# Entering the last feed-forward layer: item 0's activation ahead of a branch, and two items instead of three between the up and the down projection

## The chip, the core and the metric
The kernel runs on one core of a Trainium2 chip. The metric is the device time of one execution in microseconds (us), here the median of several runs. The engines are called as the profile calls them: PE (matrix multiply, with PEld for its weight loads), DVE (vector), ACT (scalar), POOL (GpSimd) and SP, which here only issues transfers. Each engine works through its own list of instructions in order, and waits for others by semaphores.

## What is computed
A cluster-masked attention (4 batches, 8 heads, 768 positions, 64 wide) is followed by a soft mixture of experts and by a feed-forward layer (FFN) with an odd activation:

```python
d = softmax over tokens of x @ phi;  slot_out = experts(d.T @ x)   # 32 slots of 512
x2 = softmax over slots(x @ phi) @ slot_out                         # 3072 x 512
h = x2 @ w_in                                                       # 512 -> 2048
g = h - tanh(h)
out = g @ w_out                                                     # 2048 -> 512
```

The change is at the entry of the last three lines and in their loop. The kernel never forms x2: it multiplies the 32 rows of slot_out with w_in first (`gp`, 32 x 2048), and then the softmax weights with that.

## The kernel before
The attention and the experts run to about 560 us; nothing in them is touched but the last copy of the expert outputs (`o_t`). Then the FFN works on 128 **items**: 8 groups of 384 tokens, and in each group 16 blocks `f` of 128 hidden units. For item n the work is, engine by engine:

- **up(n)**, PE, L1184: one matmul gives `u`, the 128 x 384 block of h. Its weights `gs` hold the 128 columns of block f as a high part twice and a low part (96 rows).
- **small(n)**, L1212 to L1223: ACT squares u to `y` and y to `z` (a shifted square, for a polynomial in h squared); DVE makes `gt` = u*y (L1216) and then gt = (z + c)*gt, a SCALAR_TENSOR_TENSOR that is called **STT** here (L1223). With large h another arm of the program also takes tanh itself; a flag that is computed on the chip chooses the arm (`big_h`), and in this run the arm without tanh works.
- **split(n)**, L1231 and L1233: ACT casts gt to a high part `ghi`, DVE subtracts to get the low part `glo`.
- **down(n)**, PE, L1243 to L1245: nine matmuls of 512 columns, for each of three token tiles ghi x whi, ghi x wlo and glo x whi, into the tile's accumulator `acc`. After 16 items ACT copies tiles 0 and 2 out and DVE tile 1 (`store`, L1252).

`up` and `down` of an item lie three rounds of the loop apart. In one round the order of the code is up(n), down(n-3), small(n-1), split(n-2), store(n-3).

During the first 16 items the weights are prepared too. `mix_g(q)` (PE, L1166) makes gp for four blocks; `gcopy(f)` copies it into gs (ACT L1172, then DVE L1177, and for the high part's second copy DVE L1176 in the first four blocks and POOL L1174 later); `wsplit(f)` makes `whi` on ACT (L1155) and `wlo` on POOL (L1156) from w_out. gp has one buffer, so mix_g(1) waits for the last copy of quarter 0. `u` has two PSUM buffers, ghi and glo three each.

Ahead of the branch stand mix_g(0), the flag (L1191 to L1199), gcopy(0) to (3) and wsplit(0) and (1); the arm begins with up(0).

Of the kernel before, what the change touches and what calls it, by code (L numbers as in the profile page):

```python
# [8 lines left out]
F32 = mybir.dt.float32  # L9
# [4 lines left out]
ACTF = mybir.ActivationFunctionType  # L14
ALU = mybir.AluOpType
# [313 lines left out]
def _poly():  # L329
    y = np.linspace(1e-6, H_CUT * H_CUT, 4001)  # L330
    h = np.sqrt(y)
    q = np.zeros_like(y)
    c = [1 / 3, -2 / 15, 17 / 315, -62 / 2835, 1382 / 155925, -21844 / 6081075, 929569 / 638512875]
    for k, a in enumerate(c):
        q += a * y ** k
    x = 2 * y / y[-1] - 1
    p = np.polynomial.chebyshev.cheb2poly(np.polynomial.chebyshev.chebfit(x, q, 2))
    s = 2 / y[-1]
    c2 = p[2] * s * s
    c1 = p[1] * s - 2 * p[2] * s  # L340
    c0 = p[0] - p[1] + p[2]
    r = np.sqrt(c2)
    t = c1 / (2 * r)
    return float(r), float(t), float(c0 - t * t)
# [3 lines left out]
def tile_cluster_attention_softmoe_ffn(  # L348
# [15 lines left out]
    PE, DVE, ACT, POOL, SP = nc.tensor, nc.vector, nc.scalar, nc.gpsimd, nc.sync  # L364
# [3 lines left out]
    DM = H * D  # L368
# [7 lines left out]
    HS = S // 2  # L376
    NT = S // 128
    NTOK = B * S
    KD = DM // 128
    KF = DFF // 128  # L380
    scale = 1.0 / float(D) ** 0.5
# [4 lines left out]
    keep = ctx.enter_context(tc.tile_pool(name="keep", bufs=1))  # L386
# [16 lines left out]
    ident, tri, istack, ones, afs, afb, eps, sq_b, lo_b = kviews  # L403
# [63 lines left out]
    POLY = _poly()  # L467
# [586 lines left out]
    ps_q = ctx.enter_context(tc.tile_pool(name="ps_q", bufs=1, space=PSUM, reuse_waits="tile"))  # L1054
# [26 lines left out]
    sot = keep.tile([128, KD, NS], F32, name="sot")  # L1081
# [28 lines left out]

    def o_t(gi, op):
        so = m1.tile([128, DM], F32, tag="hs", name="so")
        ACT.copy(out=so, in_=op)
        g = ps_m.tile([128, KD, 128], F32, tag="m", name="m")
        for d in range(KD):
            PE.transpose(g[:, d, :], so[:, d * 128:(d + 1) * 128], ident)
        for j in range(4):
            e = 4 * gi + j
            DVE.tensor_copy(sot[:, :, 4 * e:4 * e + 4], g[:, :, 32 * j + 4 * e:32 * j + 4 * e + 4])
# [15 lines left out]
    for f in range(F1 // 128):  # L1135
        o_mm(1, ops_[1], f)
        if f == 1:
            o_t(0, ops_[0])
        if f == 4:
            mix(3)  # L1140
    o_t(1, ops_[1])

    mctx.close()
# [4 lines left out]
    whi = ff.tile([128, KF, DM], F32R, name="whi")  # L1148
    wlo = ff.tile([128, KF, DM], F32R, name="wlo")
# [3 lines left out]
    def wsplit(f):  # L1153
        w = wu[NW + f // 4 * 4 + 2 + f // 2 % 2][:, (f % 2) * DM:(f % 2 + 1) * DM]
        ACT.copy(out=whi[:, f, :], in_=w)  # L1155
        POOL.tensor_tensor(out=wlo[:, f, :], in0=w, in1=whi.bitcast(F32)[:, f, :], op=ALU.subtract)  # L1156

    gq = {}

    def mix_g(q):  # L1160
        gq[q] = gp = ps_q.tile([128, 512], F32, tag="q", name="gp")
        for d in range(KD):
            for j in range(4):
                t = wu[NW + 4 * q + d // 2]
                c = (d % 2) * 512 + j * 128
                PE.matmul(gp[32 * j:32 * j + 32, 0:128], lhsT=sot[:, d, :], rhs=t[:, c:c + 128], start=(d == 0), stop=(d == KD - 1))  # L1166

    def gcopy(f):
        q, j = divmod(f, 4)
        fs = slice(f * 128, f * 128 + 128)  # L1170
        gpj = gq[q][32 * j:32 * j + 32, 0:128]
        ACT.copy(out=gs[0:32, fs], in_=gpj)  # L1172
        if q:
            POOL.tensor_copy(gs[32:64, fs], gf[0:32, fs])  # L1174
        else:
            DVE.tensor_copy(gs[32:64, fs], gpj)  # L1176
        DVE.tensor_tensor(out=gs[64:96, fs], in0=gpj, in1=gf[0:32, fs], op=ALU.subtract)  # L1177

    hps0 = {}

    def up(n, hps):
        g, f = items[n]
        hps[n] = ps_u.tile([128, HS], F32, tag="u", name="u")
        PE.matmul(hps[n], lhsT=gs[:, f * 128:(f + 1) * 128], rhs=cs[g // 2][0:96, g % 2 * HS:(g % 2 + 1) * HS], start=True, stop=True)  # L1184

    pctx.close()
    f3 = ctx.enter_context(tc.tile_pool(name="f3", bufs=3))
    ps_u = ctx.enter_context(tc.tile_pool(name="ps_u", bufs=2, space=PSUM, reuse_waits="tile"))
    ps_a = ctx.enter_context(tc.tile_pool(name="ps_a", bufs=5, space=PSUM, reuse_waits="tile"))
    ab = keep.tile([128, KD, NS], F32, name="ab")  # L1190
    ACT.activation(out=ab, in_=sot, func=ACTF.Abs)  # L1191
    bp = ps_a.tile([128, DM], F32, tag="acc", name="bp")
    mix_g(0)
    for d in range(KD):
        PE.matmul(bp[0:1, 0:NS], lhsT=md[:, d:d + 1], rhs=ab[:, d, :], start=(d == 0), stop=(d == KD - 1))
    bm = keep.tile([1, 1], F32, name="bm")
    DVE.tensor_reduce(out=bm, in_=bp[0:1, 0:NS], axis=AX.X, op=ALU.max)
    flag = keep.tile([1, 1], mybir.dt.int32, name="flag")
    DVE.tensor_scalar(out=flag, in0=bm, scalar1=H_CUT * (1.0 - 2.0 ** -12), scalar2=None, op0=ALU.is_gt)  # L1199
    for f in range(4):  # L1200
        gcopy(f)
        if f < 2:
            wsplit(f)
    big_h = nc.values_load(flag[0:1, 0:1], min_val=0, max_val=1)

    def ffn(any_h):
        hps, gts, gh, acc = dict(hps0), {}, {}, {}

        def small(n):
            hp = hps.pop(n)  # L1210
            y = f3.tile([128, HS], F32, tag="y", name="y", bufs=2)
            ACT.activation(out=y, in_=hp, func=ACTF.Square)  # L1212
            z = f3.tile([128, HS], F32, tag="z", name="z", bufs=2)
            ACT.activation(out=z, in_=y, func=ACTF.Square, scale=POLY[0], bias=sq_b)  # L1214
            gt = f3.tile([128, HS], F32, tag="gt", name="gt")
            DVE.tensor_tensor(out=gt, in0=hp, in1=y, op=ALU.mult)  # L1216
            if any_h:
                th = f3.tile([128, HS], F32, tag="th", name="th", bufs=1)
                ACT.activation(out=th, in_=hp, func=ACTF.Tanh)
                mk = f3.tile([128, HS], F32, tag="mk", name="mk", bufs=1)  # L1220
                POOL.tensor_scalar(out=mk, in0=y, scalar1=H_CUT * H_CUT, scalar2=None, op0=ALU.is_gt)
                DVE.tensor_tensor(out=th, in0=hp, in1=th, op=ALU.subtract)
            DVE.scalar_tensor_tensor(out=gt, in0=z, scalar=POLY[2], in1=gt, op0=ALU.add, op1=ALU.mult)  # L1223
            if any_h:
                DVE.copy_predicated(out=gt, mask=mk.bitcast(U32), data=th)
            gts[n] = gt

        def split(n):
            gt = gts.pop(n)
            a = f3.tile([128, HS], F32R, tag="ghi", name="ghi")  # L1230
            ACT.copy(out=a, in_=gt)  # L1231
            l = f3.tile([128, HS], F32R, tag="glo", name="glo")
            DVE.tensor_tensor(out=l, in0=gt, in1=a.bitcast(F32), op=ALU.subtract)  # L1233
            gh[n] = (a, l)

        def down(n):
            g, f = items[n]
            a, l = gh.pop(n)
            for t in range(3):
                if f == 0:  # L1240
                    acc[t] = ps_a.tile([128, DM], F32, tag="acc", name="acc")
                ts = slice(t * 128, (t + 1) * 128)
                PE.matmul(acc[t], lhsT=a[:, ts], rhs=whi[:, f, :], start=(f == 0), stop=False)  # L1243
                PE.matmul(acc[t], lhsT=a[:, ts], rhs=wlo[:, f, :], start=False, stop=False)  # L1244
                PE.matmul(acc[t], lhsT=l[:, ts], rhs=whi[:, f, :], start=False, stop=(f == KF - 1))  # L1245

        def store(n):
            g, f = items[n]
            if f == KF - 1:
                for t in range(3):  # L1250
                    ob = f3.tile([128, DM], F32, tag="ob", name="ob", bufs=3)
                    (DVE.tensor_copy if t == 1 else ACT.copy)(out=ob, in_=acc[t])  # L1252
                    r0 = g * HS + t * 128
                    SP.dma_start(out=out[r0:r0 + 128, :], in_=ob)

        N = len(items)
        for n in range(N + 4):
            if n < N:
                up(n, hps)
            if 4 <= n + 1 < KF:  # L1260
                gcopy(n + 1)
            if n >= 3 and n - 3 < N:
                down(n - 3)
            if 0 <= n - 1 < N:
                small(n - 1)
            if 0 <= n - 2 < N:
                split(n - 2)
            if n >= 3 and n - 3 < N:
                store(n - 3)
            if 2 <= n < KF:  # L1270
                wsplit(n)
            if n % 4 == 1 and n + 3 < KF:
                mix_g(n // 4 + 1)
# [65 lines left out]
```

## Time and profile before

| | |
|---|---|
| median of 3 runs | 861.09 us (860.93 to 864.15) |
| the profiled execution's own time | 866.37 us |
| its span, first to last instruction | 864.5 us |
| PE busy | 796.1 us (92%) |
| DVE, ACT, POOL busy | 600.5, 524.7, 396.8 us |
| mean granted clock of PE | 0.967 |

The profile is one execution, 5.3 us longer than the median; its times are measured from the first instruction. A row of the timeline gives start, duration, engine, line, operation, output <- inputs, shapes, and in brackets how long the engine had been idle and what ended that. A record can overlap the next one of its engine: the next starts while the last results are still being written.

### The profile page before, as it was taken

How to read it: one execution, taken by the hardware profiler on the slowest of the kernel's cores; microseconds unless marked ns; L12 is line 12 of the kernel's file. 1: busy time of each engine (PE TensorE's matmuls, PEld its weight loads, DVE VectorE, ACT ScalarE, POOL GpSimd, SP SyncE). 2: the span in 40 equal slices, each digit the busy share in tenths (PEclk: the TensorE clock that was granted, in tenths of full speed). 3: DMA queues.
4: the chain of work that ended last, by engine and by line, in shares of the span. 5: the costliest groups of instructions: out<-in, count | busy, mean ns of one | idle time of the engine just before them, and what ended most of it. 6: DMA issues, size and time to landing. Idle time of an engine off the chain costs nothing.

```text
span 864.5 us, 12652 instructions
## 1 busy us (share of the span) xinstructions
PE 796.1 (92%) x4327; PEld 543.5 (63%) x4327; DVE 600.5 (69%) x1017; ACT 524.7 (61%) x1085; POOL 396.8 (46%) x235
## 2 busy tenths in 40 slices
PE   1677899999999999999989979989999999999997
PEld 0343565666566656656666533368888888888885
DVE  2474676889778998789877551177767777677773
ACT  3253666658666576665656540288767767677673
POOL 1246668887887879887867721166000000000000
PEclk9798999999999999999989987989999999999999
DMA  8876788677767977678657689960000100000001
GB/s 219 187 189 174 175 230 242 170 185 186 219 174 177 220 174 205 194 201 208 181 179 275 243 341 388 382 228 2 37 37 1 38 0 38 37 1 37 1 37 40
DMA packets 49532, 135.13 MB, mean 156 GB/s; under 512 B 6866, under 2 KB 9350, under 8 KB 49460
## 3 DMA queue, kind: packets, MB, share of 16 engines
q1 hardware_dynamic: 42700, 116.29, 46.7%
q10 hardware_dynamic: 6760, 17.96, 6.9%
q8 instruction: 36, 0.59, 0.3%
q14 instruction: 36, 0.29, 0.1%
HBM read 78.55 MB, written 14.78 MB: 108 GB/s over the span
## 4 chain that ended last, share of the span: by engine, by line
PE 76%; DMA 9%; DVE 6%; SPq 3%; ACT 2%; issue 1%; POOL 1%; ACTq 0%; DVEq 0%; POOLq 0%
PE pv L671 12%; PE acc L1245 10%; PE acc L1243 10%; PE acc L1244 10%; PE st L658 7%; PE st L659 6%; PE g L605 6%; DMA pga<-in_qk_dram 4%; PE u L1184 3%; PE g L725 2%; PE h L1090 2%; DVE mx L613 2%; PE o L1109 2%; DMA xy<-pga 1%; DMA v<-in_vv_dram 1%
## 5 line engine op out<-in xcount | busy, mean ns | idle before, releaser
L676 POOL TENSOR_TENSOR es<-es,E 128x768 f32<-128x768 f32 x126 | 246.0, 1970 | 43.7 <-ACT E L663 35.8
L663 ACT ACTIVATE E<-st 128x384 f32<-128x384 f32 x384 | 174.9, 490 | 109.6 <-PE st L659 101.6
L613 DVE TENSOR_REDUCE mx<-g 128x1 f32<-128x512 f32 (+1 forms) x288 | 185.0, 682 | 69.4 <-PE g L605 68.4
L658 PE MATMUL st<-xy 112*128 112x384 f32 x384 | 146.9, 383 | 4.3 <-ACT E L663 4.3
L1245 PE MATMUL acc<-whi,glo 128*128 128x512 f32 x384 | 150.5, 392 | 0.0
L1243 PE MATMUL acc<-whi,ghi 128*128 128x512 f32 x384 | 150.2, 391 | 0.0
L1244 PE MATMUL acc<-wlo,ghi 128*128 128x512 f32 x384 | 150.0, 391 | 0.0
L671 PE MATMUL pv<-E,v 128*64 128x384 f32 x768 | 146.3, 505 | 0.0
L659 PE MATMUL st<-xy 97*128 97x384 f32 x384 | 132.0, 344 | 0.8 <-ACT xy L635 0.8
L605 PE MATMUL g<-xy 112*128 112x256 f32 (+1 forms) x384 | 104.6, 359 | 12.1 <-DMA xy<-pgb 8.5
L1216 DVE TENSOR_TENSOR gt<-u,y 128x384 f32<-128x384 f32 x128 | 71.2, 556 | 51.5 <-ACT y L1212 49.8
L658 PEld LDWEIGHTS st<-xy 112*128 112x128 f32 x384 | 73.7, 192 | 49.6 <-issue 20.5
L1212 ACT ACTIVATE y<-u 128x384 f32<-128x384 f32 x128 | 62.9, 492 | 57.5 <-PE u L1184 56.6
L671 PEld LDWEIGHTS pv<-E,v 128*64 128x64 f32 x768 | 47.7, 138 | 65.5 <-issue 62.3
L605 PEld LDWEIGHTS g<-xy 112*128 112x128 f32 x384 | 69.8, 198 | 23.3 <-issue 11.5
L1245 PEld LDWEIGHTS acc<-whi,glo 128*128 128x128 f32 x384 | 72.3, 188 | 17.8 <-DVE glo L1233 2.9
L1243 PEld LDWEIGHTS acc<-whi,ghi 128*128 128x128 f32 x384 | 72.7, 189 | 15.1
L495 POOL TENSOR_TENSOR pgb<-pga 128x768 fp32r<-128x768 f32 x31 | 58.4, 1889 | 51.6 <-DVE mx L613 24.1
L1214 ACT ACTIVATE z<-y,kt 128x384 f32<-128x384 f32 x128 | 79.2, 619 | 4.2
L1223 DVE SCALAR_TENSOR_TENSOR gt<-z,gt 128x384 f32<-128x384 f32 x128 | 71.9, 562 | 13.7 <-ACT ghi L1231 0.5
L676 POOL TENSOR_TENSOR es<-E 128x768 f32<-128x768 f32 x32 | 59.2, 1869 | 43.8 <-PE g L698 29.8
L1244 PEld LDWEIGHTS acc<-wlo,ghi 128*128 128x128 f32 x384 | 72.6, 189 | 10.2
(149 smaller groups left out, 948.8 us busy)
## 6 DMA issues: line engine op xcount, KB each, us to landing
pgw<-in_w_dram SPq DMA_DIRECT2D x64, 512.0 KB
xy<-pga SPq DMA_DIRECT2D x15, 768.0 KB
pga<-in_qk_dram ACTq DMA_DIRECT2D x14, 768.0 KB
pgc<-in_w_in_dram SPq DMA_DIRECT2D x8, 1024.0 KB
pgc<-in_w_out_dram SPq DMA_DIRECT2D x8, 1024.0 KB
xy<-pga SPq DMA_DIRECT2D x18, 384.0 KB
v<-in_vv_dram ACTq DMA_DIRECT2D x16, 384.0 KB
xy<-pga SPq DMA_DIRECT2D x32, 192.0 KB
```

What stands on the lines that cost most here:

```text
L605: PE.matmul(g[:, o:o + kn], lhsT=x[0:112, QX, qt * 128:(qt + 1) * 128], rhs=x[0:112, KX, k0:k0 + kn], start=True, stop=True)
L613: DVE.tensor_reduce(out=m[:, m0:m0 + w], in_=g.rearrange("p (a b) -> p a b", a=w), axis=AX.X, op=ALU.max)
L658: PE.matmul(s, lhsT=x[0:112, KX, ks], rhs=x[0:112, QX, qs], start=True, stop=False)
L659: PE.matmul(s, lhsT=x[0:97, KY, ks], rhs=x[0:97, QY, qs], start=False, stop=True)
L663: ACT.activation(out=et[p, kb, c][:, h, :], in_=s, func=ACTF.Exp, scale=scale)
L671: PE.matmul(pv[p, c][64 * h:64 * h + 64, :], lhsT=vt[p][:, kb, h, :], rhs=et[p, kb, c][:, h, :], start=(kb == 0), stop=(kb == NKB - 1))
L676: add_engine(p, kb, c).tensor_tensor(out=es[p][:, c], in0=et[p, 0, c] if kb == 1 else es[p][:, c], in1=et[p, kb, c], op=ALU.add)
L1214: ACT.activation(out=z, in_=y, func=ACTF.Square, scale=POLY[0], bias=sq_b)
L1223: DVE.scalar_tensor_tensor(out=gt, in0=z, scalar=POLY[2], in1=gt, op0=ALU.add, op1=ALU.mult)
L1243: PE.matmul(acc[t], lhsT=a[:, ts], rhs=whi[:, f, :], start=(f == 0), stop=False)
L1244: PE.matmul(acc[t], lhsT=a[:, ts], rhs=wlo[:, f, :], start=False, stop=False)
L1245: PE.matmul(acc[t], lhsT=l[:, ts], rhs=whi[:, f, :], start=False, stop=(f == KF - 1))
```

## The change
It has four parts, and the parts of the FFN's entry belong together.

1. wsplit(0) is issued before the flag's first step. The flag's last two steps come behind gcopy(0) on DVE, and up(0) and small(0) stand ahead of the branch, outside both arms. gcopy(2), gcopy(3) and wsplit(1) go into the arms.
2. gp is one tile, with 128 columns of its own for each quarter, so that mix_g(q) no longer waits for the copies of the quarter before it. In the built program ACT's copy gs(2) waits for the last matmul of mix_g(1).
3. A round of the loop is up(n), gcopy(n+1), down(n-2), split(n-1), small(n), store(n-2), wsplit(n). The nine matmuls of down(0) alone are sorted by kind: first the three ghi x whi.
4. In the second o_t, ACT copies the first half of the columns and DVE the second. In the built program DVE's half waits for ACT's.

```diff
     def o_t(gi, op):
         so = m1.tile([128, DM], F32, tag="hs", name="so")
-        ACT.copy(out=so, in_=op)
+        if gi:
+            ACT.copy(out=so[:, 0:DM // 2], in_=op[:, 0:DM // 2])
+            DVE.tensor_copy(so[:, DM // 2:DM], op[:, DM // 2:DM])
+        else:
+            ACT.copy(out=so, in_=op)
...
-    gq = {}
+    gq = ps_q.tile([128, 512], F32, tag="q", name="gp")
     def mix_g(q):
-        gq[q] = gp = ps_q.tile([128, 512], F32, tag="q", name="gp")
...
-                PE.matmul(gp[32 * j:32 * j + 32, 0:128], lhsT=sot[:, d, :], rhs=t[:, c:c + 128], start=(d == 0), stop=(d == KD - 1))
+                PE.matmul(gq[32 * j:32 * j + 32, q * 128:q * 128 + 128], lhsT=sot[:, d, :], rhs=t[:, c:c + 128], start=(d == 0), stop=(d == KD - 1))
...
+    wsplit(0)
     ACT.activation(out=ab, in_=sot, func=ACTF.Abs)
...
+    gcopy(0)
+    up(0, hps0)
     DVE.tensor_reduce(out=bm, in_=bp[0:1, 0:NS], axis=AX.X, op=ALU.max)
-    flag = keep.tile([1, 1], mybir.dt.int32, name="flag")
     DVE.tensor_scalar(out=flag, in0=bm, scalar1=H_CUT * (1.0 - 2.0 ** -12), scalar2=None, op0=ALU.is_gt)
-    for f in range(4):
-        gcopy(f)
-        if f < 2:
-            wsplit(f)
+    gcopy(1)
+    y0, z0, gt0 = y_z(0, hps0.pop(0), "gt0")
+    DVE.scalar_tensor_tensor(out=gt0, in0=z0, scalar=POLY[2], in1=gt0, op0=ALU.add, op1=ALU.mult)
     big_h = nc.values_load(flag[0:1, 0:1], min_val=0, max_val=1)
...
-        for n in range(N + 4):
+        if any_h:
+            up(0, hps)
+            small(0)
+        else:
+            gts[0] = gt0
+        up(1, hps)
+        mix_g(1)
+        split(0)
+        wsplit(1)
+        gcopy(2)
+        small(1)
+        for n in range(2, N + 2):
             if n < N:
                 up(n, hps)
-            if 4 <= n + 1 < KF:
+            if n + 1 < KF:
                 gcopy(n + 1)
-            if n >= 3 and n - 3 < N:
-                down(n - 3)
-            if 0 <= n - 1 < N:
-                small(n - 1)
-            if 0 <= n - 2 < N:
-                split(n - 2)
-            if n >= 3 and n - 3 < N:
-                store(n - 3)
-            if 2 <= n < KF:
+            down(n - 2)
+            if n <= N:
+                split(n - 1)
+            if n < N:
+                small(n)
+            store(n - 2)
+            if n < KF:
                 wsplit(n)
```

How the instructions stand is shown at three places. First PE at the branch (TENSOR_LOAD reads the flag), before:

```order
L1166 MATMUL gp<-pgw,sot 32x128 x16
L1195 MATMUL bp<-ab,md 1x32 x4
L1204 TENSOR_LOAD flag
L1275 COMPARE_AND_BRANCH
L1184 MATMUL u<-csm,gs 128x384 x2
L1166 MATMUL gp<-pgw,sot 32x128 x16
L1184 MATMUL u<-csm,gs 128x384 x2
L1243 MATMUL acc<-whi,ghi 128x512
```

And of the change:

```order
L1169 MATMUL gp<-pgw,sot 32x128 x16
L1199 MATMUL bp<-ab,md 1x32 x4
L1187 MATMUL u<-csm,gs 128x384
L1219 TENSOR_LOAD flag
L1295 COMPARE_AND_BRANCH
L1187 MATMUL u<-csm,gs 128x384
L1169 MATMUL gp<-pgw,sot 32x128 x16
L1187 MATMUL u<-csm,gs 128x384
L1256 MATMUL acc<-whi,ghi 128x512 x3
```

One up is now ahead of the branch, and three instead of four ups are ahead of the first down. The second place is DVE during the first 16 items; the numbers tell the buffers of one item from those of the next. Before:

```order
L1216 TENSOR_TENSOR gt_9959<-u_9914,y_9955 128x384
L1223 SCALAR_TENSOR_TENSOR gt_9959<-z_9957,gt_9959 128x384
L1233 TENSOR_TENSOR glo_9964<-gt_9932,ghi_9962 128x384
L1177 TENSOR_TENSOR gs_5750<-gp_9870,gs_5750 32x128
L1216 TENSOR_TENSOR gt_9986<-u_9941,y_9982 128x384
L1223 SCALAR_TENSOR_TENSOR gt_9986<-z_9984,gt_9986 128x384
L1233 TENSOR_TENSOR glo_9991<-gt_9959,ghi_9989 128x384
```

And of the change:

```order
L1209 TENSOR_TENSOR gt_9959<-u_9937,y_9955 128x384
L1233 SCALAR_TENSOR_TENSOR gt_9959<-z_9957,gt_9959 128x384
L1180 TENSOR_TENSOR gs_5751<-gp_5754,gs_5751 32x128
L1243 TENSOR_TENSOR glo_9980<-gt_9959,ghi_9978 128x384
L1209 TENSOR_TENSOR gt_9986<-u_9964,y_9982 128x384
L1233 SCALAR_TENSOR_TENSOR gt_9986<-z_9984,gt_9986 128x384
```

Before, the subtraction that reads gt_9959 (glo_9991) stands behind the whole next item's gt and STT; now it (glo_9980) stands ahead of them. The third place is ACT in the same items, before:

```order
L1231 CAST ghi_9962<-gt_9932 128x384
L1155 CAST whi_5751<-pgw_5492 128x512
L1172 CAST gs_5750<-gp_9870 32x128
L1212 ACTIVATE y_9982<-u_9941 128x384
L1214 ACTIVATE z_9984<-y_9982,kt_77 128x384
L1231 CAST ghi_9989<-gt_9959 128x384
```

And of the change:

```order
L1241 CAST ghi_9951<-gt_9932 128x384
L1205 ACTIVATE y_9955<-u_9937 128x384
L1207 ACTIVATE z_9957<-y_9955,kt_77 128x384
L1159 CAST whi_5752<-pgw_5485 128x512
L1175 CAST gs_5751<-gp_5754 32x128
L1241 CAST ghi_9978<-gt_9959 128x384
```

The cast of an item (ghi_9989 before, ghi_9978 now, both from gt_9959) used to follow y and z of the next item, and now stands ahead of them. The first 16 items are used for the place because whi and gs stand between there; behind them the order of ghi, y, z and of glo, gt, STT is the same without those.

## Rows read from the trace of the kernel before

**Rows 1.** The page's head.

```profile
span 864.5 us, 12652 instructions
```

**Rows 2.** Windows: start:end, length, busy (x instructions) of PE, PEld, DVE, ACT, POOL; clock; DMA.

```profile
567.00:573.00 6.00, 5.98 (x44) 4.35 (x37) 5.06 (x11) 5.80 (x14) 2.94 (x3) 0.58 1.05 383
650.00:700.00 50.00, 50.00 (x226) 41.73 (x225) 36.50 (x71) 35.02 (x70) 0.00 (x0) 1.00 0.04 17
```

**Rows 3.** Timeline of all engines, from the branch to the end of down(0).

```profile
564.14 0.41 PE L1184 MATMUL u<-csm,gs 96*128 96x384 f32 x1 [1.28 <-ACT gs L1172]
...
566.31 0.30 DVE L1177 TENSOR_TENSOR gs<-gp,gs 32x128 fp32r<-32x128 f32 x1
...
566.66 1.94 PE L1166 MATMUL gp<-pgw,sot 128*32 128x128 f32 x32 [1.33 <-DVE gs L1177]
...
568.16 0.56 DVE L1223 SCALAR_TENSOR_TENSOR gt<-z,gt 128x384 f32<-128x384 f32 x1
...
568.75 0.51 ACT L1231 CAST ghi<-gt 128x384 fp32r<-128x384 f32 x1
...
569.72 0.63 PE L1243 MATMUL acc<-whi,ghi 128*128 128x512 f32 x1
...
572.84 0.34 PE L1184 MATMUL u<-csm,gs 96*128 96x384 f32 x1
```

**Rows 4.** Timeline of ACT and DVE behind the first group's store.

```profile
608.85 0.59 ACT L1252 COPY ob<-acc 128x512 f32<-128x512 f32 x1 [0.77 <-PE acc L1245]
...
609.33 0.50 ACT L1212 ACTIVATE y<-u 128x384 f32<-128x384 f32 x1
609.86 0.56 DVE L1216 TENSOR_TENSOR gt<-u,y 128x384 f32<-128x384 f32 x1 [1.00 <-ACT y L1212]
...
610.39 0.50 ACT L1231 CAST ghi<-gt 128x384 fp32r<-128x384 f32 x1
...
610.53 0.56 DVE L1223 SCALAR_TENSOR_TENSOR gt<-z,gt 128x384 f32<-128x384 f32 x1
...
610.79 0.48 ACT L1212 ACTIVATE y<-u 128x384 f32<-128x384 f32 x1
...
611.00 0.55 DVE L1233 TENSOR_TENSOR glo<-gt,ghi 128x384 fp32r<-128x384 f32 x1
...
611.47 0.55 DVE L1216 TENSOR_TENSOR gt<-u,y 128x384 f32<-128x384 f32 x1
```

**Rows 5.** Timeline of one item in the middle of the FFN.

```profile
700.40 0.34 PE L1184 MATMUL u<-csm,gs 96*128 96x384 f32 x1
...
700.77 0.49 ACT L1212 ACTIVATE y<-u 128x384 f32<-128x384 f32 x1 [0.67 <-PE u L1184]
...
702.62 0.34 PE L1184 MATMUL u<-csm,gs 96*128 96x384 f32 x1
```

**Rows 6.** Timeline of one engine each: POOL and what DVE and ACT do beside it.

```profile
576.02 0.62 ACT L1155 CAST whi<-pgw 128x512 fp32r<-128x512 f32 x1
...
576.78 1.30 POOL L1156 TENSOR_TENSOR wlo<-pgw,whi 128x512 fp32r<-128x512 f32 x1 [0.32 <-ACT whi L1155]
...
599.96 0.55 DVE L1233 TENSOR_TENSOR glo<-gt,ghi 128x384 fp32r<-128x384 f32 x1
...
600.23 1.44 POOL L1156 TENSOR_TENSOR wlo<-pgw,whi 128x512 fp32r<-128x512 f32 x1 [0.60 <-ACT whi L1155]
...
601.34 0.75 DVE L1223 SCALAR_TENSOR_TENSOR gt<-z,gt 128x384 f32<-128x384 f32 x1
...
433.81 1.92 POOL L676 TENSOR_TENSOR es<-E 128x768 f32<-128x768 f32 x1
...
433.99 2.15 DVE L536 TENSOR_TENSOR eq<-pgb,am 128x384 bf16<-128x384 f32 x1
...
L536 DVE TENSOR_TENSOR eq<-pgb,am x16: 518/560/2152, 9.7 to 434.0; 128x384 bf16<-128x384 f32 x16
```

**Rows 7.** Timeline of PE, its last matmul.

```profile
858.21 0.39 PE L1245 MATMUL acc<-whi,glo 128*128 128x512 f32 x1
```

More of the change, by code (lines that the diff above doesn't have):

```diff
@@ L1170, in gcopy @@
         fs = slice(f * 128, f * 128 + 128)
-        gpj = gq[q][32 * j:32 * j + 32, 0:128]
+        gpj = gq[32 * j:32 * j + 32, q * 128:q * 128 + 128]
         ACT.copy(out=gs[0:32, fs], in_=gpj)
@@ L1196, in tile_cluster_attention_softmoe_ffn, with y_z @@
     bm = keep.tile([1, 1], F32, name="bm")
+    flag = keep.tile([1, 1], mybir.dt.int32, name="flag")
+    def y_z(n, hp, tag="gt"):
+        y = f3.tile([128, HS], F32, tag="y", name="y", bufs=2)
+        ACT.activation(out=y, in_=hp, func=ACTF.Square)
+        z = f3.tile([128, HS], F32, tag="z", name="z", bufs=2)
+        ACT.activation(out=z, in_=y, func=ACTF.Square, scale=POLY[0], bias=sq_b)
+        gt = f3.tile([128, HS], F32, tag=tag, name="gt", bufs=3 if tag == "gt" else 1)
+        DVE.tensor_tensor(out=gt, in0=hp, in1=y, op=ALU.mult)
+        return y, z, gt
+    gcopy(0)
+    up(0, hps0)
     DVE.tensor_reduce(out=bm, in_=bp[0:1, 0:NS], axis=AX.X, op=ALU.max)
-    flag = keep.tile([1, 1], mybir.dt.int32, name="flag")
     DVE.tensor_scalar(out=flag, in0=bm, scalar1=H_CUT * (1.0 - 2.0 ** -12), scalar2=None, op0=ALU.is_gt)
-    for f in range(4):
-        gcopy(f)
-        if f < 2:
-            wsplit(f)
+    gcopy(1)
+    y0, z0, gt0 = y_z(0, hps0.pop(0), "gt0")
+    DVE.scalar_tensor_tensor(out=gt0, in0=z0, scalar=POLY[2], in1=gt0, op0=ALU.add, op1=ALU.mult)
     big_h = nc.values_load(flag[0:1, 0:1], min_val=0, max_val=1)
@@ L1210, in small @@
             hp = hps.pop(n)
[L1211 to L1216, printed above, removed]
+            y, z, gt = y_z(n, hp)
             if any_h:
@@ L1238, in down @@
             a, l = gh.pop(n)
-            for t in range(3):
-                if f == 0:
+            if f == 0:
+                for t in range(3):
                     acc[t] = ps_a.tile([128, DM], F32, tag="acc", name="acc")
[L1242 to L1245, printed above, removed]
+            mms = [(t, k) for t in range(3) for k in range(3)]
+            if n == 0:
+                mms.sort(key=lambda m: m[1])
+            for t, k in mms:
+                PE.matmul(acc[t], lhsT=(l if k == 2 else a)[:, t * 128:(t + 1) * 128], rhs=(wlo if k == 1 else whi)[:, f, :], start=(f == 0 and k == 0), stop=(f == KF - 1 and k == 2))
         def store(n):
```

## The prediction, made before the change was run
> **What bounds the kernel now.** I read the page's head first: the span of the profiled execution is 864.5 us [rows 1], 1.87 short of its own 866.37, and that time is 5.3 above the median of 861.09. All sums below are made inside this execution, as a shift of its last matmul, and the shift is then added to the median. Next the windows: in the middle of the FFN PE is busy 50.00 of 50 us at a granted clock of 1.00, DVE 36.5 and ACT 35.0 [rows 2]. So PE is the bound there, and the item in the timeline takes 702.62 - 700.40 = 2.22 us [rows 5]. DVE and ACT have a quarter of the time free, but a busy share says nothing on how long they need one after the other. That is what the change touches, so the rest is read from timelines: the entry [rows 3], the hops between ACT and DVE [rows 4], POOL beside DVE [rows 6] and the end [rows 7].
>
> **The loop after the change.** Before, STT(n-1) stands ahead of glo(n-2) on DVE, and ghi(n-2) behind y and z of n-1 on ACT. An item crosses between the engines, but its split doesn't hold up the next item's STT. After it, ACT does ghi(n-1), y(n), z(n) and DVE glo(n-1), gt(n), STT(n). STT(n) therefore stands behind glo(n-1), which needs ghi(n-1), which needs STT(n-1): a closed loop, once around for each item. Its legs:
> - STT to ghi: 568.75 - 568.16 = 0.59 [rows 3].
> - ghi to glo: an ACT operation of 0.50 and the hop to DVE, as y at 609.33 to gt at 609.86, 0.53 [rows 4].
> - glo to gt on DVE: 611.47 - 611.00 = 0.47 [rows 4].
> - gt to STT, which reads it: 610.53 - 609.86 = 0.67 [rows 4].
>
> They sum to 2.26 (each is rounded to 0.01; I take 2.255), against PE's 2.22. y and z of n lie inside (y at 0.40 after ghi, 610.39 to 610.79, and 1.06 for y and z together, 609.33 to 610.39 [rows 4]), so ACT is ready when STT wants z. The loop becomes the bound by some 0.035 an item. From item 16 to 127 that is 111 turns, 250.3 us.
>
> **Group edges.** store's two ACT copies, 0.48 each (608.85 to 609.33 [rows 4]), now stand between z(n) and ghi(n). From ghi to ghi ACT then needs 0.40 + 1.06 + 0.96 = 2.42, 0.17 over 2.255. Seven edges make 1.2 us. Nothing hides it, since the loop has no slack.
>
> **The first 16 items.** There POOL works beside DVE, and two operations that read only SBUF hold each other up. The eq of L536 takes 0.56 in the median and 2.15 when it starts at 433.99 beside POOL's es (433.81 to 435.73); STT at 601.34 takes 0.75 in place of 0.56 beside wlo (600.23 to 601.67) [rows 6]. Both end about 0.41 after a point 0.15 ahead of POOL's end, as though they began there. The other way round, that wlo took 1.44 and not 1.30, with glo at 599.96 ahead of it. So a wlo holds a later STT or glo for about 1.15 after its start, and waits itself for about 0.41 after the start of an earlier one. gt and the copies into gs read PSUM and are not held in these rows. In before such a hold falls on an operation that isn't in a loop; now it lengthens the loop.
>
> wlo's place: y 0.40 after ghi, whi 1.06 behind, wlo 0.76 after whi (576.02 to 576.78 [rows 6]), so 2.22 after ghi or 2.81 after STT. Two patterns are possible.
> - **A**: STT is first, wlo gets in at STT + 0.41 and holds until + 1.56. glo, which is due at 0.59 + 0.53 = 1.12, starts at 1.56, gt at 2.03, STT at 2.69. The next wlo is due at 2.81, behind that STT again: this repeats, by a margin of 0.12, with a turn of 2.69.
> - **B**: wlo starts when STT has just ended (+ 0.56) and holds until 1.71; glo 1.71, gt 2.18, the next STT due at 2.84. The next wlo, due at 2.81, is 0.03 ahead and holds this STT to 3.96. The turn behind that is free again, 2.25. The mean is 3.1.
>
> Which runs hangs on 0.03 to 0.12 us, less than I can add up. I take the middle, 2.9, and keep 2.69 and 3.1 as bounds. Thirteen turns (items 3 to 16) make 37.7.
>
> The Trainium skill, in "SBUF — State Buffer", section "Who interferes with whom", says that a DVE instruction with two SBUF inputs and a GpSimd instruction that reads SBUF exclude each other for a whole instruction. The rows agree in kind and differ by 0.15 at the end; by the page a hold would last all of 1.30, pattern A would turn in 2.84, and the sum would be 13 x 0.15 = 2.0 us higher.
>
> **The entry.** u(0), y, z, gt and STT of item 0 now run while the flag is made and read. The flag comes behind two DVE copies of 0.30 each (566.31 [rows 3]), so the branch is about 0.6 late, and u(1) behind it starts at 564.14 + 0.6, about 564.8. mix_g(1) no longer waits for the last copy at 566.31 + 0.30; before it began at 566.66 and took 1.94 [rows 3]. Now it follows u(1) and ends at about 566.9. gs(2) waits for that: an ACT copy and two DVE copies, about 0.9, then hops; u(2) at about 567.9 and down(0) at 568.3, against 569.72 [rows 3]. PE is at the lower level there (granted clock 0.58 in 567 to 573 [rows 2]; 0.5 is 1.2 GHz): nine matmuls of 512 columns take 9 x 0.43 = 3.9, and u(3) starts at 572.2; with the 3.12 of before (569.72 to 572.84 [rows 3]) at 571.4. Before, the u that follows down(0) starts at 572.84, and PE has one u less left: u is 384 of an item's 4992 columns, 0.17. So the gain for PE is 0.5, and 1.3 at the other bound. This is all that the part can bring, however early item 0's activation is, since from there PE has a full list.
>
> Costed at nothing: wsplit(0) ahead of the absolute values (they are wanted only behind mix_g(0), 16 matmuls pairs on PE; uncovered it would be one ACT and one POOL operation, 0.76 and 1.30); the branch on ACT and DVE, beside PE's u(1) and mix_g(1); the order inside down(0), which lets PE start with ghi alone and whose nine matmuls are the same. The second o_t's halves are chained in the built program, ACT's and then DVE's, so its transposes start about when they did: 0, at most 0.1 either way. No transfer moves against another on SP.
>
> **The sum.** STT(3) is y + gt + STT behind u(3): 572.2 + 0.37 (700.40 to 700.77 [rows 5]) + 0.53 + 0.67 = 573.8. Then 37.7, 250.3 and 1.2 give STT(127) at 863.0. The end: ghi 0.59, glo 0.53, 0.55 for it [rows 4] and a hop of 0.05 (566.31 + 0.30 to 566.66 [rows 3]) to the third matmul, and six more of 2.22 x 512/4992 = 0.23: 3.1. The last matmul starts at 866.1, against 858.21 [rows 7]: + 7.9. On the median, 861.1 + 7.9 = **868.9 us** (874.2 for a profiled execution like this one). With A alone it is 866.2, with B alone 871.5.
>
> **Rivals.**
> - **No hold in the loop**: STT and glo slip in between wlo's, because wlo comes later than 2.81, behind the gs copies on ACT and POOL. Then the weight stage goes at PE's pace, 2.22 and two mix_g of some 0.97 (half of 1.94 at the full clock) over 13 items, 2.37. 13 turns are 30.8, the last matmul 859.2, + 1.0: 862.1. For it: STT at 601.34 lost only 0.19. Against: wlo needs 1.3 of every turn, and glo and STT are 1.13 to 1.7 apart, so there is hardly a gap that it fits.
> - **PE stays the bound** (the other side): the loop turns in 2.22 or less, because a leg is 0.04 shorter when nothing else is in flight, and holds eat only the slack. Then the entry's 0.5 to 1.3 is all that is left: 859.8 to 860.6, not slower. It is decided at a turn of 2.22. Against: four rows would have to be wrong in the same direction, and the holds fall in the first 16 items even so; for: PE can trail, as ghi and glo are ready some 1.7 us ahead of their down.
> - **The clock comes back sooner**: with down(0) 1.4 us earlier and fewer gaps ahead of it, nine matmuls at the full clock would take 2.05 and not 3.9, 1.8 less: 867.1 by my sum, 858.4 if PE is the bound too.
>
> **How the numbers follow.** The loop with holds, A, B or a mixture: 0.63, 865 to 872. No hold in the loop: 0.20, near 862. PE the bound: 0.12, 858.4 to 860.6. Something longer than B: 0.05. The early clock (0.25, in any of them) shifts each by less than 2. The range of 861 to 872 leaves out about 0.15. A measurement of this kernel tells some 0.5%, 4.3 us, from no change: faster is under 856.8, which only PE as the bound, an early clock and edges that get cheaper together would reach, 0.04; slower is above 865.4, most of the first case and the last, 0.63; the rest 0.33.
>
> **What would show it.** Between 650 and 700 us u's start 2.25 to 2.26 apart, PE has gaps that glo or ghi end, and its busy time falls under 50; if they are 2.22 apart, the loop isn't the bound. Between 572 and 610 STT or glo rows of 0.9 to 1.7 and wlo rows of 1.4 to 1.7, with turns of 2.7 (A) or 2.25 and 3.9 in alternation (B); if all are 0.56 and 1.30, the holds were wrong. down(0) starts at about 568.3, the first u after it at 571.4 to 572.2, and the last matmul at 866. What would make it wrong most easily: legs shorter by 0.04, or holds that fall elsewhere.

## The result and the profile after

The changed kernel is slower: 871.78 us (median of 16 runs, 867.41 to 876.88) against 862.86 for the kernel before in 16 runs. The ratio is 1.0098, with a 95% interval of 1.0072 to 1.0124. The forecast was + 7.9 us, 0.92%; its 868.9 us counted from the 861.09 of three runs before, so 871.78 lies close under the upper end of its range of 861 to 872.

Single runs of one kernel lie about 1% apart, and so do the starts of the FFN in the traces. So I compare a **stretch**: from the start of the first gp matmul (mix_g(0)) to the start of the last matmul. Each stretch here is read from one traced execution of its kernel. Behind item 16 they repeat well: the eight kernels with the changed order take 252.97 to 253.71 there. How much their first part varies from execution to execution no run shows. First the start of it before; the last matmul is in [rows 7]. Timeline of PE of the kernel before, as in the rows above:

```profile
561.57 1.08 PE L1166 MATMUL gp<-pgw,sot 128*32 128x128 f32 x32 [0.51 <-DVE sot L1119]
```

That makes 858.21 - 561.57 = 296.64 us. Now the head of the page of the changed kernel, which answers to [rows 1]:

```profile
span 870.1 us, 12655 instructions
```

The timeline of its PE at the entry, which answers to [rows 3]:

```profile
559.61 1.08 PE L1169 MATMUL gp<-pgw,sot 128*32 128x128 f32 x32 [0.51 <-DVE sot L1123]
...
562.94 0.54 PE L1187 MATMUL u<-csm,gs 96*128 96x384 f32 x1 [0.72 <-ACT y L1205]
563.42 1.94 PE L1169 MATMUL gp<-pgw,sot 128*32 128x128 f32 x32
566.46 0.66 PE L1187 MATMUL u<-csm,gs 96*128 96x384 f32 x1 [1.11 <-DVE gs L1180]
566.92 1.49 PE L1256 MATMUL acc<-whi,ghi 128*128 128x512 f32 x3
...
570.38 0.34 PE L1187 MATMUL u<-csm,gs 96*128 96x384 f32 x1
```

Counted from the first gp matmul, down(0) starts at 7.31 (before: 569.72 - 561.57 = 8.15) and the first u behind it at 10.77 (before: 11.27). So that u comes 0.5 earlier. But four u's stood ahead of down(0) before and three do now; the one that is left is worth 0.17, so PE's gain at the entry is 0.33. All of the loss comes later. The same kernel's DVE timeline, STT of items 3, 16 and 127, and PE's last matmul:

```profile
572.22 0.56 DVE L1233 SCALAR_TENSOR_TENSOR gt<-z,gt 128x384 f32<-128x384 f32 x1
...
608.44 0.56 DVE L1233 SCALAR_TENSOR_TENSOR gt<-z,gt 128x384 f32<-128x384 f32 x1
...
861.65 0.56 DVE L1233 SCALAR_TENSOR_TENSOR gt<-z,gt 128x384 f32<-128x384 f32 x1
...
864.90 0.39 PE L1256 MATMUL acc<-whi,glo 128*128 128x512 f32 x1
```

The stretch is 864.90 - 559.61 = 305.29, 8.65 more than before. (The last matmul is only 6.69 later than before on the clock of the profile, since this run reached the FFN 1.96 earlier.) 13 turns of STT take 36.22, 111 turns 253.21. One turn in the middle, timeline of PE, PEld, DVE and ACT:

```profile
699.89 0.56 DVE L1233 SCALAR_TENSOR_TENSOR gt<-z,gt 128x384 f32<-128x384 f32 x1
...
700.49 0.52 ACT L1241 CAST ghi<-gt 128x384 fp32r<-128x384 f32 x1 [0.72 <-DVE gt L1233]
...
701.03 0.56 DVE L1243 TENSOR_TENSOR glo<-gt,ghi 128x384 fp32r<-128x384 f32 x1 [0.58 <-ACT ghi L1241]
...
701.10 0.34 PE L1187 MATMUL u<-csm,gs 96*128 96x384 f32 x1
...
701.51 0.55 DVE L1209 TENSOR_TENSOR gt<-u,y 128x384 f32<-128x384 f32 x1
701.65 0.19 PEld L1256 LDWEIGHTS acc<-whi,glo 128*128 128x128 f32 x1 [0.18 <-DVE glo L1243]
...
702.17 0.56 DVE L1233 SCALAR_TENSOR_TENSOR gt<-z,gt 128x384 f32<-128x384 f32 x1
...
703.38 0.34 PE L1187 MATMUL u<-csm,gs 96*128 96x384 f32 x1
```

Each bracket names the leg ahead of it: ghi waits for gt, glo for ghi, and PE's weight load for glo. The legs are 0.60, 0.54, 0.48 and 0.66; the turn is 2.28 here, 2.271 in the median of turns 20 to 126, against PE's 2.22. In the first 16 items, timeline of DVE, ACT and POOL:

```profile
600.22 0.56 DVE L1233 SCALAR_TENSOR_TENSOR gt<-z,gt 128x384 f32<-128x384 f32 x1
600.32 1.62 POOL L1160 TENSOR_TENSOR wlo<-pgw,whi 128x512 fp32r<-128x512 f32 x1 [0.64 <-ACT whi L1159]
...
600.82 0.51 ACT L1241 CAST ghi<-gt 128x384 fp32r<-128x384 f32 x1 [0.36 <-DVE gt L1233]
...
601.36 0.49 ACT L1205 ACTIVATE y<-u 128x384 f32<-128x384 f32 x1
601.36 0.99 DVE L1243 TENSOR_TENSOR glo<-gt,ghi 128x384 fp32r<-128x384 f32 x1 [0.25 <-ACT ghi L1241]
...
602.39 0.56 DVE L1209 TENSOR_TENSOR gt<-u,y 128x384 f32<-128x384 f32 x1
...
603.05 0.56 DVE L1233 SCALAR_TENSOR_TENSOR gt<-z,gt 128x384 f32<-128x384 f32 x1
603.14 1.63 POOL L1160 TENSOR_TENSOR wlo<-pgw,whi 128x512 fp32r<-128x512 f32 x1 [0.64 <-POOL gs L1177]
```

This is pattern A: STT is just ahead of wlo, wlo is stretched to 1.62, glo to 0.99 (it ends 0.41 behind wlo, 602.35 to 601.94), and the turn is 2.83. STT is never held in these turns: each takes 0.56. The windows, which answer to [rows 2]:

```profile
567.00:573.00 6.00, 6.00 (x22) 4.88 (x21) 5.32 (x11) 4.98 (x12) 2.30 (x3) 0.76 0.97 356
650.00:700.00 50.00, 50.00 (x221) 39.03 (x220) 35.17 (x68) 34.41 (x68) 0.00 (x0) 1.00 0.06 21
```

PE is still shown 50.00 of 50 us busy, although its items are 2.27 apart: only the counts, 221 matmuls and 226, tell. The weight loads do show the waits (groups of lines in that window, busy and mean ns, then idle before and what ended it), after:

```profile
L1256 PEld LDWEIGHTS acc<-whi,glo 128*128 128x128 f32 x66 | 12.4, 187 | 6.0 <-DVE glo L1243 4.1
```

and before:

```profile
L1245 PEld LDWEIGHTS acc<-whi,glo 128*128 128x128 f32 x68 | 12.8, 188 | 3.0 <-DVE glo L1233 0.4
```

### The profile page after: what moved, and what is told of

Its sections match the earlier page's. It is cut to its first block, busy times and chain, and to the rows that moved or that the text cites. A ratio compares the mean times of both kernels' runs of the same rounds, so it can differ in the third digit from the quotient of the medians.

```text
span 870.1 us, 12655 instructions
## 1 busy us (share of the span) xinstructions
PE 801.5 (92%) x4327; PEld 531.9 (61%) x4327; DVE 610.7 (70%) x1018; ACT 526.9 (61%) x1085; POOL 399.3 (46%) x235
## 4 chain that ended last, share of the span: by engine, by line
PE 72%; DMA 10%; DVE 7%; ACT 4%; POOL 2%; issue 2%; SPq 2%; ACTq 0%; DVEq 0%; POOLq 0%
PE acc L1256 29%; PE pv L671 11%; PE st L658 7%; PE st L659 5%; PE g L605 5%; DMA pga<-in_qk_dram 4%; PE u L1187 3%; PE g L725 2%; PE h L1090 2%; DVE mx L613 2%; POOL es L676 2%; PE o L1109 2%; DMA xy<-pga 2%; DMA xy<-pgb 1%; DMA v<-in_vv_dram 1%
## 5 line engine op out<-in xcount | busy, mean ns | idle before, releaser
L1256 PE MATMUL acc<-whi,glo 128*128 128x512 f32 x384 | 153.9, 402 | 0.0
L1243 DVE TENSOR_TENSOR glo<-gt,ghi 128x384 fp32r<-128x384 f32 x128 | 77.5, 606 | 66.6 <-ACT ghi L1241 65.7
L1241 ACT CAST ghi<-gt 128x384 fp32r<-128x384 f32 x128 | 65.8, 514 | 81.7 <-DVE gt L1233 80.7
```

What stands on the lines that cost most here:

```text
L1256: PE.matmul(acc[t], lhsT=(l if k == 2 else a)[:, t * 128:(t + 1) * 128], rhs=(wlo if k == 1 else whi)[:, f, :], start=(f == 0 and k == 0), ...
```

## The experiments

The theory is that the loss is the closed loop (turns of 2.27) and the holds between wlo and DVE that lengthen it in the first 16 items. The rivals are that a lag of two items is too short in any order, or that the entry or the gp tile costs something. A ratio can be told from 1 where its interval leaves 1 out; differences of less than 1 us between two stretches rest on one trace each.

| run | median us | ratio to before (95%) | stretch | STT 3 to 16 | STT 16 to 127 |
|---|---|---|---|---|---|
| before | 862.86 | | 296.64 | 30.10 | 248.11 |
| changed | 871.78 | 1.0098 (1.0072 to 1.0124) | 305.29 | 36.22 | 253.21 |
| e1 small first | 864.36 | 1.0008 (0.9976 to 1.0041) | 299.36 | 32.53 | 249.69 |
| e2 loop of before | 864.76 | 1.0017 (0.9986 to 1.0048) | 299.31 | 32.82 | 247.07 |
| e3 no wlo | 866.52 | 1.0036 (1.0006 to 1.0067) | 302.20 | 33.12 | 253.20 |
| e4 loop alone | 877.57 | 1.0172 (1.0110 to 1.0234) | 310.39 | 40.02 | 253.21 |
| e5 closed, lag three | 872.19 | 1.0103 (1.0051 to 1.0155) | 306.08 | 36.21 | 253.42 |
| e6 woven | 861.05 | 0.9968 (0.9943 to 0.9993) | 295.64 | 32.08 | 246.42 |
| e7 loop and gp tile | 872.63 | 1.0098 (1.0060 to 1.0135) | 306.79 | 36.23 | 253.39 |
| e8 wlo twice | 880.00, one run | | 313.16 | 43.57 | 253.71 |
| e9 woven, entry of before | 864.24 | 0.9974 (0.9947 to 1.0001) | 296.25 | 31.83 | 246.42 |
| e10 first rows | 874.36, one run | | 308.71 | 40.02 | 253.10 |
| e11 first rows, ACT | 874.45, one run | | 309.20 | 40.34 | 252.97 |

The ratios are to runs of before on the same chip, whose medians were 863.60 (e1 to e4), 864.12 (e5 to e8) and 865.05 (e9 to e11).

**e1**, small(n) ahead of split(n-1).

```diff
-                split(n - 1)
-            if n < N:
-                small(n)
+            if n < N:
+                small(n)
+            if n <= N:
+                split(n - 1)
```

> The changed kernel with one swap in a round of the loop: small(n) stands ahead of split(n-1), everything else is as changed. 'Stretch' is from the first gp matmul to the last matmul: 296.6 us before, 305.3 changed. Theory of the closed loop (STT, ghi, glo, gt, STT once around for each item): the swap opens it, u's in the middle are 2.22 apart again, the stretch falls to 296 to 299 and the time to that of before, -0.3% to +0.3%. Rival, a lag of two items is itself too short (down waits for a split that was made too late, in whatever order): u's stay above 2.25 apart, PE waits for glo in each item, stretch 303 or more.

The time is that of before, and 6 of the 8.65 us of the stretch are back, so the order matters. But the rival has a part of it: u's are not all 2.22 apart. Timeline of PE, PEld and DVE of e1:

```profile
691.31 0.55 DVE L1243 TENSOR_TENSOR glo<-gt,ghi 128x384 fp32r<-128x384 f32 x1
691.49 0.34 PE L1187 MATMUL u<-csm,gs 96*128 96x384 f32 x1
...
691.92 0.19 PEld L1256 LDWEIGHTS acc<-whi,glo 128*128 128x128 f32 x1
...
693.74 0.34 PE L1187 MATMUL u<-csm,gs 96*128 96x384 f32 x1
...
695.96 0.34 PE L1187 MATMUL u<-csm,gs 96*128 96x384 f32 x1
```

They are 2.25 and 2.22 apart in turn. glo's first weight load starts 0.06 behind its end (691.86), as it does where PE waits for it in the changed kernel (701.59 to 701.65). With small(n) first as a whole, glo is made last in its round, and for a lag of two that seems just too late. The profile puts only 0.4 us of the weight loads' waits in 650 to 700 down to glo, as in before, so this cause is argued here; e6, which makes glo earlier and has every u from item 16 on at 2.22, bears it out.

**e2**, the new entry with the loop of before.

```diff
-        split(0)
         wsplit(1)
         gcopy(2)
-        small(1)
-        for n in range(2, N + 2):
+        for n in range(2, N + 3):
...
-            down(n - 2)
+            if n >= 3:
+                down(n - 3)
...
+                small(n - 1)
...
+                split(n - 2)
```

> The new entry, gp tile and second o_t, but the loop of before: lag of three, small(n-1) ahead of split(n-2). Closed loop theory: everything lost was lost in the loop, so the stretch is 296.1 (the 0.5 of the entry gained), the time within 0.3% of before. Rival, the entry or the one gp tile costs something (PE and the copies at one PSUM tile, the branch): the stretch is 300 or more and the loss lies ahead of item 16.

The middle is as before (2.22), and the time can't be told from before. But the gain of the entry isn't there, and the expected stretch of 296.1 did not come: it is 2.7 longer than before. With a lag of three u(3) stands ahead of down(0) and waits for gt(1); the u behind down(0) is at 12.81 and not 11.27, which is 1.5 of it. The rest arises up to item 16, and its cause stays open. So here the entry pays only where down(0) follows u(2).

**e3**, without wlo. **e8**, wlo twice.

```diff
-        POOL.tensor_tensor(out=wlo[:, f, :], in0=w, in1=whi.bitcast(F32)[:, f, :], op=ALU.subtract)
+        if f < 2:
+            POOL.tensor_tensor(out=wlo[:, f, :], in0=w, in1=whi.bitcast(F32)[:, f, :], op=ALU.subtract)
...
-rhs=(wlo if k == 1 else whi)[:, f, :]
+rhs=(wlo[:, f % 2, :] if k == 1 else whi[:, f, :])
```

> The changed kernel without POOL's wlo for blocks 2 to 15; the matmuls that want it read the wlo of blocks 0 and 1, so only the low part of the weights is left out. Theory that wlo and glo hold each other up in the first 16 items: no glo of 0.99 is left, 13 turns of STT (3 to 16) take 30 to 32 us and not 36.2, behind them the turn stays 2.27, the stretch is 299 to 301. Rival, the longer turns of that stage come from the ACT and DVE copies into gs and from whi: 35 us or more, stretch 304 to 305.

```diff
         POOL.tensor_tensor(out=wlo[:, f, :], in0=w, in1=whi.bitcast(F32)[:, f, :], op=ALU.subtract)
+        if 4 <= f:
+            POOL.tensor_tensor(out=wlo[:, f, :], in0=w, in1=whi.bitcast(F32)[:, f, :], op=ALU.subtract)
```

> The changed kernel with wlo computed twice on POOL in blocks 4 to 15, to the same values. Hold theory: the second wlo is put into the loop as well, either behind glo, where it holds STT (turns of 3.1), or ahead of it, where glo waits for both (turns of 4.0 to 4.2); the 13 turns take 40 to 54 us and not 36.2. Rival, POOL's work lies beside the loop and the 0.99 of glo has another cause: 36 to 37.

Without wlo the long glo is gone. Groups of lines of e3, DVE, 573 to 604:

```profile
L1244 DVE TENSOR_TENSOR glo<-gt,ghi 128x384 fp32r<-128x384 f32 x13 | 7.3, 559 | 3.4 <-ACT ghi L1242 2.6
```

The 13 turns fall by 3.1 and not by the 4 to 6 that I expected (33.12 lies between the two ranges, as the stretch does), because rounds with a mix_g on PE take 3.63 and 3.08 there (ACT's copy of the new gp waits for it, and ghi stands behind that copy), and the others still go around the closed loop, most in 2.27 or 2.39. Behind item 16 nothing changes (253.20). With wlo twice the turns of that stage grow to some 3.5, and both operations are held; timeline of e8, POOL and DVE:

```profile
596.28 1.28 POOL L1160 TENSOR_TENSOR wlo<-pgw,whi 128x512 fp32r<-128x512 f32 x1
...
596.64 1.34 DVE L1245 TENSOR_TENSOR glo<-gt,ghi 128x384 fp32r<-128x384 f32 x1 [0.27 <-ACT ghi L1243]
...
597.64 1.48 POOL L1162 TENSOR_TENSOR wlo<-pgw,whi 128x512 fp32r<-128x512 f32 x1
...
598.55 0.99 DVE L1235 SCALAR_TENSOR_TENSOR gt<-z,gt 128x384 f32<-128x384 f32 x1
```

glo slips in between the two wlo, and the second holds STT. POOL's work is in the loop: 43.57 and not 36.22.

**e4**, the loop alone on the kernel before. **e7**, the same with the one gp tile.

```diff
-            if n >= 3 and n - 3 < N:
-                down(n - 3)
+            if n >= 2 and n - 2 < N:
+                down(n - 2)
             if 0 <= n - 1 < N:
-                small(n - 1)
...
+                split(n - 1)
+            if n < N:
+                small(n)
```

> The kernel before with the order of the loop alone changed (down(n-2), split(n-1), small(n)); entry, gp tiles and o_t as before. Closed loop theory: the same loss as in the whole change, less what the new entry gives back, so the stretch is 305 to 306.5 and the time 0.9% to 1.3% above before. Rival, the new entry makes the loss: stretch 296 to 299, the time that of before.

> The kernel of e4 (entry of before, new loop), with the one gp tile in four parts added. e4 lost 5 us more than the whole change. If that was mix_g waiting for the copies of the quarter before it, the two waits (1.43 and 2.61) are gone and the stretch is 305 to 307. Rival, it was the activation of item 0 ahead of the branch: 309 to 311.

The loop alone loses more than the whole change, 13.75 in the stretch, where I expected 8.4 to 9.9; the intervals of the two ratios overlap. mix_g waits for the copies of the quarter before. Timeline of PE of e4:

```profile
575.57 1.08 PE L1166 MATMUL gp<-pgw,sot 128*32 128x128 f32 x32 [1.43 <-DVE gs L1177]
...
588.47 1.93 PE L1166 MATMUL gp<-pgw,sot 128*32 128x128 f32 x32 [2.61 <-DVE gs L1177]
```

With gp's own columns (e7) there are no such waits, and 3.6 come back. (One late round of e4 also has an STT held to 1.66, which e7 has not; it is part of the 3.6.) The entry gives the other 1.5 (306.79 to 305.29). So the entry and the gp tile are worth 5.1 beside this loop.

**e5**, the order of the change with a lag of three.

```diff
-        for n in range(2, N + 2):
+        for n in range(2, N + 3):
...
-            down(n - 2)
+            if n >= 3:
+                down(n - 3)
             if n <= N:
                 split(n - 1)
             if n < N:
                 small(n)
```

> The changed kernel with its order of split(n-1) ahead of small(n), but down and store three items behind, as before, with four buffers of ghi and glo. Closed loop theory: the order alone makes the loss, however far off down is. STT's turn in the middle stays 2.27, the stretch is 305 to 307.5, the time 0.8% to 1.3% above before. Rival, the lag of two is what costs: u's are 2.22 apart again, the stretch is 296 to 300.

The loss stays: STT turns in 2.27, item by item, so the closed order costs this by itself, however late down is. u's own spacing is 2.22 in the median, as the rival had it, but PE gathers its waits at one place, the group's edge, where the next accumulator waits for ACT's copies, which stand in the slow loop. The waits of PE in e5, 650 to 700 (us in total, times, longest):

```profile
PE acc L1256 <- ACT ob L1263: 0.7, 1, 0.7
```

In the trace the u's at an edge are 3.13 to 3.18 apart, and 15 items of 2.22 with one of these come to the same as 16 turns of the loop. So one sign of the rival came, its stretch of 296 to 300 did not.

**e6**, the two woven. **e9**, the same on the entry of before with the one gp tile.

```diff
-                split(n - 1)
...
-                small(n)
...
+            ACT.activation(out=y, in_=hp, func=ACTF.Square)
...
+            ACT.copy(out=a, in_=gp)
...
+            ACT.activation(out=z, in_=y, func=ACTF.Square, scale=POLY[0], bias=sq_b)
...
+            DVE.tensor_tensor(out=gt, in0=hp, in1=y, op=ALU.mult)
...
+            DVE.tensor_tensor(out=l, in0=gp, in1=a.bitcast(F32), op=ALU.subtract)
...
+            DVE.scalar_tensor_tensor(out=gt, in0=z, scalar=POLY[2], in1=gt, op0=ALU.add, op1=ALU.mult)
```

(hp is u of item n; gp is here gt of item n-1.)

> The changed kernel, lag of two, with small(n) and split(n-1) woven: ACT does y(n), ghi(n-1), z(n), and DVE gt(n), glo(n-1), STT(n). By the rows the way around one item is 1.7 (STT, ghi, z, STT), under PE's 2.22, and glo is ready some 0.5 earlier than in e1, where small(n) went first as a whole and u's stayed 2.24 apart. Closed loop theory: u's 2.22 apart, the stretch 296 to 298, the time that of before, within 0.3%. Rival, a lag of two is too short in any order: u's at 2.24 or more, 299 or more.

> The woven loop of e6 on the entry of before (item 0's activation behind the branch), with the one gp tile. Theory: the entry is worth what the first u behind down(0) is earlier, about 0.9 (at 10.9 and 11.8 from the first gp matmul in e6 and e7), and no more, so the stretch is 296 to 297.5 and the time 0% to 0.3% under before. Rival, the entry is what made e6 faster than before: the stretch is 298 or more, the time that of before or above.

e6 is the fastest kernel here, 0.3% under before, with an interval clear of 1, and the stretch is 1.0 shorter. A lag of two is not too short. Groups of lines, PEld of e6, 650 to 700: no wait for glo is left.

```profile
L1272 PEld LDWEIGHTS acc<-whi,glo 128*128 128x128 f32 x68 | 12.8, 188 | 2.7
```

The edges are gone as well: in before one u in 16 comes 0.25 late, in e6 none does. e9 keeps most of this on the old entry; its stretch is 0.6 longer than e6's. The two times (864.24 and 861.05) can't be told apart by their ratios, 0.9974 and 0.9968.

**e10** and **e11**, other rows of gp.

```diff
-        gpj = gq[32 * j:32 * j + 32, q * 128:q * 128 + 128]
+        gpj = gq[0:32, q * 128:q * 128 + 128]
```

(In e11 only in ACT's copy. In e10 the weights of a quarter's other three blocks are so left out.)

> The changed kernel, in which the copies into gs read the rows of each quarter's first block for all four blocks (rows 0 to 31 of gp), so that the other blocks' weights are left out. In the changed kernel, turns of STT in which the first block of a quarter is copied or none take 2.70, the others 2.82. If rows further down in gp make the copy or what follows it later, all turns are 2.70 now and the 13 turns take 35.1. Rival, it is the order or the waits of those rounds, whatever rows are read: 36.2 again.

> As e10, but only ACT's copy reads the first block's rows; DVE's subtraction reads each block's own. If ACT's read of the rows further down makes the 0.12, all turns are 2.70 here too; if DVE's does, 2.82 is left, as it is by the rival of e10.

Neither of the times came, since the stage ran in pattern B. But the rows answer the question. Timeline of e10, POOL and DVE:

```profile
586.05 1.29 POOL L1160 TENSOR_TENSOR wlo<-pgw,whi 128x512 fp32r<-128x512 f32 x1 [0.41 <-POOL gs L1177]
586.06 1.69 DVE L1233 SCALAR_TENSOR_TENSOR gt<-z,gt 128x384 f32<-128x384 f32 x1
...
588.33 0.56 DVE L1243 TENSOR_TENSOR glo<-gt,ghi 128x384 fp32r<-128x384 f32 x1 [0.27 <-ACT ghi L1241]
...
588.81 0.55 DVE L1209 TENSOR_TENSOR gt<-u,y 128x384 f32<-128x384 f32 x1
...
589.46 0.56 DVE L1233 SCALAR_TENSOR_TENSOR gt<-z,gt 128x384 f32<-128x384 f32 x1
...
592.28 1.67 DVE L1233 SCALAR_TENSOR_TENSOR gt<-z,gt 128x384 f32<-128x384 f32 x1
```

wlo starts 0.01 ahead of STT and holds it to 1.69. A held STT's record begins with its wait, so a turn is read from end to end here: 587.75 to 590.02 is 2.27, to 593.95 another 3.93. That is B as predicted (2.25 and 3.96). 13 turns take 40.02 and 40.34.

And of e11, ACT, DVE and POOL:

```profile
571.00 0.51 ACT L1241 CAST ghi<-gt 128x384 fp32r<-128x384 f32 x1 [0.26 <-DVE gt L1233]
571.42 0.49 ACT L1205 ACTIVATE y<-u 128x384 f32<-128x384 f32 x1
...
573.20 1.29 POOL L1160 TENSOR_TENSOR wlo<-pgw,whi 128x512 fp32r<-128x512 f32 x1 [0.52 <-POOL gs L1177]
573.23 1.68 DVE L1233 SCALAR_TENSOR_TENSOR gt<-z,gt 128x384 f32<-128x384 f32 x1
...
588.02 0.56 DVE L1243 TENSOR_TENSOR glo<-gt,ghi 128x384 fp32r<-128x384 f32 x1 [0.26 <-ACT ghi L1241]
...
588.61 0.56 DVE L1209 TENSOR_TENSOR gt<-u,y 128x384 f32<-128x384 f32 x1
```

- **The 0.12 of a turn** comes from the rows that DVE's copy reads. In e11, where DVE still reads each block's own rows, gt starts 0.59 behind glo, and the turns without a hold take 2.39 (2.27 for a quarter's first block); in e10, where it reads rows 0 to 31, they are 0.48 and 2.27. The order is the same in both, so the rival of e10 falls.
- **ACT has the same**: where its copy reads rows 32 and up, y starts 0.53 to 0.54 behind the ghi ahead of it (changed kernel, 600.82 to 601.36), otherwise 0.42 (e11, 571.00 to 571.42). Why it costs this, no run shows.
- **This chose the pattern** in e11. STT is 2.23 behind the ghi of the item before it both there (571.00 to 573.23) and in the changed kernel (600.82 to 603.05). wlo, which follows ACT's whi, is 2.20 behind it in e11 and 2.32 in the changed kernel, so it moved from behind STT to ahead of it.

## Why the prediction was right

Counted from the first gp matmul, in us:

| term | predicted | measured |
|---|---|---|
| first u behind down(0) | 10.6 | 10.77 |
| STT(3) behind it | 1.6 | 1.84 |
| 13 turns | 37.7 | 36.22 |
| 111 turns and edges | 251.5 | 253.21 |
| end | 3.1 | 3.25 |
| sum, the stretch | 304.5 | 305.29 |

- **The loop** was right: e5 differs from e2 in the order within a round (and a fourth buffer of ghi and glo), and its stretch is 6.8 longer. The leg sum of 2.255 was 0.016 short of 2.271: 1.8 us in 111 turns, the largest error behind item 16. Six of seven edges took 0.14 and not 0.17.
- **The holds** were right in kind: e3 takes them away, e8 adds to them. Pattern A ran, with turns of 2.70 and 2.83 (the 0.12 wasn't in my 2.69), and B runs in e10 and e11 as predicted (2.27 and 3.93 in alternation, 40.02 and 40.34 in sum, predicted 40.3). That the choice hangs on less than can be added up was so: 0.12 moved it. But taking the holds away gives 3.1 us and not the 6.9 that lie between 37.7 and the rival's 30.8: the turns of e3 take 33.12 / 13 = 2.55 in the mean and not 2.37. That rival let the stage go at PE's 2.22, but the loop stays closed without the holds: most turns take 2.27 or 2.39, and two mix_g come on top.
- **Luck**: 37.7 was the middle of two patterns of which one ran. A alone was 13 x 2.69 = 35.0, and the 0.12 of nine turns, which I did not have, brought it near the middle. That the 13 turns came 1.5 below the forecast and the 111 turns with their edges 1.7 above it, and that the two nearly cancel, was luck too: the sum is better than its terms. (Its last step is rounded down: 861.09 and 7.9 make 869.0.)
- **The Trainium skill**, "SBUF — State Buffer", section "Who interferes with whom", has a DVE instruction with two SBUF inputs contend with a GpSimd instruction that reads SBUF, and calls the port pair that they share an exclusive lock, which whoever issues first has for the whole instruction. By an estimate from that, A would have turned in 2.84 at least. The trace agrees in kind and not in length: glo ends 0.41 behind wlo, as in [rows 6], and turns of 2.70 occur, so the shorter hold was the better figure.
- **The entry** gave PE 0.33 where the sum had 0.5. That it came so near is two errors that nearly cancel: u(2) behind gs(2) came 0.5 later than I had it, down(0) with it, and the nine matmuls took 3.46 (granted clock 0.76 in 567 to 573) and not 3.9.
- **gp's own columns** I priced only at mix_g(1). Beside this loop they are worth 3.6 (e4, e7), since there mix_g(2) and (3) would wait.
- **The second o_t** gave nothing: the transposes start 1.17 and not 1.35 behind the last o matmul, but the first gp matmul 2.57 and not 2.52.
- **The rivals** fell: no hold in the loop, since every glo of items 2 to 15 takes 0.98 or more; PE the bound, by the turn of 2.271; the early clock, by nine matmuls of 3.46 where it had 2.05.
- One sign that I named was wrong: PE's busy time in the middle did not fall under 50.00, though PE waited.

## What to carry to other kernels

Before two steps of a pipeline change places, follow one item's result through the engines' lists and ask whether the next item's start now stands behind it. If so, the sum of the hops is a lower bound of the round, whatever the busy shares say: here 2.27 against 2.22, with DVE and ACT busy under three quarters of the time. The cure need not be a longer lag: an order in which each engine does a step of the next item between two steps of this one (e6) took out the loop and the stalls at the group edges.

## What the runs showed of the hardware

A stage in which DVE and POOL hold each other up has two steady patterns here, and a start of wlo 0.12 us earlier chose the other: 36.2 or 40.0 to 40.3 us for the same 13 items. A held instruction's record includes its wait, so its end tells more than its start. Behind an ACT or DVE copy that reads rows 32 and up of a PSUM tile, y or gt started 0.11 to 0.12 later than behind one that reads rows 0 to 31 (y 0.54 and 0.42 behind ghi, gt 0.59 and 0.48 behind an unheld glo). And records of matmuls that overlap can cover waits: PE was shown 50.00 of 50 us busy with 221 matmuls as with 226, and the waits stood with the weight loads.
